# Loading the first slab of q's weights in two column halves, and x's first tile in two halves on two queues

## The chip, the cores and the metric

The kernel runs on one core of one Trainium2 chip. The metric is the time of one execution on the device in microseconds (us); the figure for a kernel is the median of several executions. Times such as "at 10.13" are us from the start of the profiled span.

The engines are named as the profile names them: PE multiplies matrices (PEld is its weight load), DVE, ACT and POOL work on vectors, SP only issues loads and stores. A name with q (SPq, ACTq) is that engine's instruction queue, in which DMA issues stand.

## The reference

Two branches work on `xn`, the layer-normed x of 2048 rows and 576 columns, and the result joins them:

```python
xn = layernorm(x)
q  = xn @ wq                       # 576 -> 32 heads of 128
p  = softmax(q @ k.T * Dh**-0.5)   # 16 key heads, last 512 rows of the caches
s  = (p @ v) @ wo                  # 4096 -> 576
h  = gelu(layernorm(xn) @ w1)      # its four quarters are shifted by 1, -1, 2, -2 rows
x1 = xn + shifted(h) @ w2
b  = x1 + gelu(layernorm(x1) @ w3) @ w4      # 576 -> 4608 -> 576
out = x + s * silu(b)
```

All arrays are bf16. `wq` has 576 rows and 4096 columns, `w4` 4608 rows and 576 columns.

## The kernel before

**Stages.** Rows go in four blocks of 512 (`QB`), a block is four tiles of 128 rows (`TB`). Stage A is attention with the first part of the second branch: a unit u is one head of one block, 128 units in all. For each unit PE makes q (`stage_q`, L460), the scores (`stage_s`, L481), their product with v (`stage_v`, L498), and the products with `wo`, `w1` and `w2` are placed between them. ACT takes the exponentials (L483), DVE copies and scales. Stage B, from about 539 us, is `w3`, GELU, `w4`: `up` (L894) and `down` (L931), over nine slabs of 512 columns of `w3` with the 512 rows of `w4` that belong to them (`load_w(i)`, L845 to L852). The order on PE, SP and POOL is written out by hand in both stages; for DVE and ACT it is so in the start and in stage B, and a planner sets it in the rest of stage A.

**The start.** All of this must be done before the first unit:

- x's first four tiles are loaded, two by SP and two by ACT (L316).
- `ln1_first` (L362 to L392) norms them. DVE takes mean and variance of tiles 0, 1 and 2 by `bn_stats` in two halves of 288 columns (L379). ACT takes those of tile 3 in two passes over it (L372, L373). Behind these two passes, in ACT's order, stands the square root for tiles 0 and 1 (L382); DVE's reciprocal (L389) needs it, and then applies the norm to each tile (L390).
- PE transposes the tiles (L404) and the first four key heads (L420), the transposes of a pair of tiles and of a pair of heads taking turns. DVE and ACT copy the five transposed chunks to `xT_b` (L410, L412): chunks 0, 1 and 4 DVE, chunks 2 and 3 ACT.
- `stage_q(0)` and `stage_q(1)` multiply them with the first two heads' weights, five matmuls each, one for each chunk of 128 rows of `wq` (the fifth has 64). A slab of `wq_b` holds four heads, 512 columns; `stage_q(2)` and `stage_q(3)` read its second half.

SP issues in this order: x tiles 0 and 1, key heads 0 and 1, key heads 2 and 3, the first slab of `wq` (L266, and its last 64 rows L269), v for two heads, the second slab of `wq`, v for two more heads, four more key heads. ACT issues x tiles 2 and 3 and then works.

**Semaphores of the loads.** Loads and stores issued by SP and ACT take eight semaphores in turn. In the trace each one from the ninth on waits, before it is issued, for the landing of the one that had its semaphore before: the first load of v waits for that of x's tile 2, the second for that of tile 0.

**From A to B.** `load_w` runs on SP from 511 us, each load behind such a wait or behind the release of memory that stage A used. For slabs 0 to 4 the 576 KB of `w4` come in one load, for slabs 5 to 8 in two. At the end of stage A ACT stores the last block of s (L544), also with one of the eight semaphores, then loads its table and takes the first GELU (L912).

Of the kernel before, what the change touches and what calls it, by code (L numbers as in the profile page):

```python
# [8 lines left out]
P = 128  # L9
# [22 lines left out]
def kernel(  # L32
# [14 lines left out]
    nc = tc.nc  # L47
# [3 lines left out]
    _, S, D = A_x.shape  # L51
    _, Hkv, Sk, Dh = A_k_cache.shape
# [13 lines left out]
    NF = D // P  # L66
    DR = D - NF * P
# [12 lines left out]
    x2 = A_x.rearrange("b s d -> (b s) d")  # L80
# [128 lines left out]
    with ExitStack() as actx:  # L209
# [9 lines left out]
        wq_b = [res.tile([P, NDC, 4 * Dh], BF16, name=f"wq_b{i}") for i in range(NWQ)]  # L219
# [26 lines left out]
        def x_tile(b):  # L246
            if b < 2:
                xt = hb_pool.tile([P, 5, QB + 2 * PAD], BF16, name="hb")[:].rearrange("p a b -> p (a b)")
            else:
                xt = x1_pool.tile([P, TB, D], BF16, name="x1")[:].rearrange("p a b -> p (a b)")  # L250
            return xt[:, 0:TB * D].rearrange("p (t d) -> p t d", t=TB)
# [10 lines left out]
        def load_wq(j, eng=None):  # L262
            eng = eng or nc.gpsimd
            w = wq_b[j % NWQ]
            c0 = (j % 8) * 4 * Dh
            eng.dma_start(out=w[:, 0:NF, :],  # L266
                              in_=A_wq[0:NF * P, c0:c0 + 4 * Dh].rearrange("(kc p) m -> p kc m", p=P))
            if j < PLAIN // 4:
                eng.dma_start(out=w[0:DR, NF, :], in_=A_wq[NF * P:D, c0:c0 + 4 * Dh])  # L269
                return  # L270
            last = A_wq[NF * P:D, c0:c0 + 4 * Dh].rearrange("p (j two m) -> p j two m", two=2, m=Dh)
            for k in range(2):
                eng.dma_start(out=w[k * DR:(k + 1) * DR, NF, 0:2 * Dh].rearrange("p (j m) -> p j m", j=2),
                              in_=last[:, :, k, :])
# [4 lines left out]
        def load_k(i, eng=None, step=4):  # L279
            kst_t[i] = x1_pool.tile([P, TB, D], BF16, name="x1")  # L280
            dst = kst_t[i][:].rearrange("p a b -> p (a b)")[:, 0:4 * W].rearrange("p (g a) -> p g a", g=4)
            for g in range(0, 4, step):
                (eng or nc.gpsimd).dma_start(
                    out=dst[:, g:g + step, :],
                    in_=A_k_cache[0, 4 * i + g:4 * i + g + step, K0:, :].rearrange("g (p kc) d -> p g (kc d)", p=P))

        def load_v(i, eng=None):
            for g in (2 * i, 2 * i + 1):
                (eng or nc.gpsimd).dma_start(out=v_sb[:, g, :, 0:Dh],
                                             in_=A_v_cache[0, g, K0:, :].rearrange("(p kc) d -> p kc d", p=P))  # L290
# [20 lines left out]

        x_t[0] = []
        x_first = x_tile(0)
        for tt in range(TB):
            xt = x_first[:, tt, :]
            (nc.sync if tt < 2 else nc.scalar).dma_start(out=xt, in_=x2[tt * P:(tt + 1) * P, :])  # L316
            x_t[0].append(xt)
        for w in (xn_b[0], xnn_b):
            nc.gpsimd.memset(w[:, :, D:], 0.0)
# [1 line left out]
            nc.gpsimd.memset(w[DR:, NF, :], 0.0)  # L321
        with tc.manual_schedule(engines={SP}):
            load_k(0, nc.sync, 2)
            load_wq(0, nc.sync)
            load_v(0, nc.sync)
            load_wq(1, nc.sync)
            load_v(1, nc.sync)
            load_k(1, nc.sync)
# [466 lines left out]
        with tc.manual_schedule(engines={SP, POOL, PE}):  # L795
            for u in range(0, max(max(fill), max(pe_fill)) + 1):
                atoms = pe_fill.get(u, []) + [fn for v, g in pe_late if v == u for fn in prep_k(g)]
                n = len(atoms)
# [23 lines left out]
    with ExitStack() as bctx:  # L822
# [5 lines left out]
        WS = 4  # L828
# [14 lines left out]
        def load_w(i):  # L843
            c0 = i * WS * P
            nc.sync.dma_start(out=w3_s[i][:, :, :],  # L845
                              in_=B_w3[0:NF * P, c0:c0 + WS * P].rearrange("(kc p) f -> p kc f", p=P))
            last = B_w3[NF * P:D, c0:c0 + WS * P].rearrange("p (j two m) -> p j two m", two=2, m=P)
            for k in range(2):
                nc.sync.dma_start(out=w3r_s[i][k * DR:(k + 1) * DR, :, :], in_=last[:, :, k, :])
            for k in range(0, WS, WS if i < 5 else WS // 2):  # L850
                n = WS if i < 5 else WS // 2
                nc.sync.dma_start(out=w4_s[i][:, k:k + n, :],  # L852
                                  in_=B_w4[c0 + k * P:c0 + (k + n) * P, :].rearrange("(fc p) d -> p fc d", p=P))

        with tc.issue_after(last_t[0].ins):
            for i in range(NSL):
                load_w(i)
# [236 lines left out]
        with tc.manual_schedule(engines={PE, DVE, ACTE, SP}):  # L1094
# [20 lines left out]
            tt = TB - 1  # L1115
# [11 lines left out]
    with tc.If(flag > 0):  # L1127
        nc.sync.dma_start(out=g_dram[(NT - 1) * P:NT * P, :], in_=g_last)
        with ExitStack() as gctx:
# [19 lines left out]
            with tc.For_i(0, NT, 1) as t:  # L1149
                tok = bass.ds(t * P, P)  # L1150
                xt = work.tile([P, D], BF16, name="r_x")
# [8 lines left out]
                for h in range(Hq):  # L1160
                    g = h // REP
                    if h % REP == 0:
                        k_nat = work.tile([P, KCH, Dh], BF16, name="r_k")
                        nc.sync.dma_start(out=k_nat[:],
                                          in_=A_k_cache[0, g, K0:, :].rearrange("(kc p) d -> p kc d", p=P))
                        v_g = work.tile([P, KCH, Dh], BF16, name="r_v")
                        nc.sync.dma_start(out=v_g[:],
                                          in_=A_v_cache[0, g, K0:, :].rearrange("(kc p) d -> p kc d", p=P))
# [16 lines left out]
                    p = work.tile([P, W], BF16, name="r_p")  # L1185
# [63 lines left out]
```

## Time and profile before

| | |
|---|---|
| three executions | 829.02, 829.21, 830.68 us |
| median | 829.21 us |
| the profiled execution | 829.95 us, of it the span 828.2 us |
| PE busy | 819.9 us, 99% of the span |
| granted PE clock | full in all 40 slices |
| DVE, ACT, POOL busy | 472.4, 456.0, 96.1 us |
| DMA | 83.81 MB, 101 GB/s over the span |

The profile is of one execution. "Idle before" is the time in which an engine did nothing before an instruction, with what ended it. The chain of work is followed back from the last instruction; time of an engine that is not on the chain costs nothing by itself.

The trace has a landing mark for each DMA from each of the 16 DMA engines; a load has landed when the last has come. In the start these are, issue to landing:

| load | queue | issued | landed |
|---|---|---|---|
| x tile 0 | SP | 0.75 | 3.50 |
| x tile 2 | ACT | 0.75 | 3.72 |
| x tile 1 | SP | 1.21 | 4.16 |
| x tile 3 | ACT | 1.19 | 4.37 |
| keys of heads 0, 1 | SP | 1.68 | 7.78 |
| keys of heads 2, 3 | SP | 2.15 | 8.59 |
| first slab of wq | SP | 2.67 | 10.09 |
| its last 64 rows | SP | 3.18 | 10.48 |
| v, two heads | SP | 3.80, 4.44 | 10.88, 11.48 |
| second slab of wq | SP | 5.12 | 14.07 |

From the keys on one of the 16 engines is behind the rest: 15 had finished the keys of heads 0 and 1 by 6.01 and the first slab of wq by 8.60.

### The profile page before, as it was taken

To read this page: it belongs to the slowest core of one execution; us is meant where nothing else is said; L and a number is where in the kernel's file an instruction comes from. 1 tells how busy PE (TensorE), PEld (TensorE's weight loads), DVE (VectorE), ACT (ScalarE), POOL (GpSimd) and SP (SyncE) were. 2 spreads that over 40 slices of the span, in tenths; PEclk is the share of its full clock that TensorE was granted. 3 is DMA by queue.
4 is the path that set the end of the run, shared out by engine and by line. 5 is a ranking of instruction groups with operands and counts; after the bars stand their busy time and mean duration, and the time that the engine had idled before them with its cause. 6 is when DMAs were issued, how large, how long until landed. Compare 5 with 4: busy or idle time off the path is not lost.

```text
span 828.2 us, 19604 instructions
## 1 busy us (share of the span) xinstructions
PE 819.9 (99%) x7974; PEld 470.0 (57%) x7974; DVE 472.4 (57%) x1431; ACT 456.0 (55%) x821; POOL 96.1 (12%) x163
## 2 busy tenths in 40 slices
PE   8999999999999999999999999999999999999997
PEld 5666654655564565655466555555555555555555
DVE  5878645678885357964346774044246626645323
ACT  7888853588773368984457983033233423334610
POOL 4353223010100111110001100000000000000000
PEclk9999999999999999999999999999999999999999
DMA  7998992263472145762045454992000311220101
GB/s 196 196 189 175 192 171 76 80 125 71 107 140 56 42 91 125 139 137 49 13 81 128 103 106 94 314 332 42 2 16 30 91 44 45 48 87 16 45 15 40
DMA packets 141217, 83.81 MB, mean 101 GB/s; under 512 B 107888, under 2 KB 134000, under 8 KB 141120
## 3 DMA queue, kind: packets, MB, share of 16 engines
q1 hardware_dynamic: 130464, 53.01, 32.1%
q0 software_dynamic: 9408, 28.15, 12.9%
q8 instruction: 64, 1.05, 0.5%
q10 hardware_dynamic: 1248, 1.33, 0.5%
q14 instruction: 33, 0.27, 0.1%
HBM read 49.17 MB, written 9.29 MB: 71 GB/s over the span
## 4 chain that ended last, share of the span: by engine, by line
PE 98%; DMA 1%; ACT 0%; SPq 0%; DVE 0%; issue 0%; ACTq 0%
PE po L498 14%; PE ph L894 14%; PE psq L460 13%; PE sc L481 13%; PE pswo L522 13%; PE pm L931 11%; PE pm L1101 4%; PE ph L574 3%; PE pm L894 2%; PE psx L625 2%; PE pswr L522 2%; PE pr L931 2%; PE psq L445 1%; DMA wq_b<-in_A_wq_dram 1%; PE sc L445 1%; PE pr L1101 0%
## 5 line engine op out<-in xcount | busy, mean ns | idle before, releaser
L483 ACT ACTIVATE pT<-sc 128x512 bf16<-128x512 f32 x512 | 285.3, 598 | 104.9 <-PE sc L481 98.2
L481 PE MATMUL sc<-qT,kT 128*128 128x512 bf16 x512 | 172.8, 379 | 0.0
L498 PEld LDWEIGHTS <-pT 128*128 128x128 bf16 x2048 | 134.4, 98 | 55.0 <-issue 10.6
L498 PE MATMUL po<-v_sb,pT 128*128 128x129 bf16 x2048 | 158.3, 220 | 0.1
L460 PE MATMUL psq<-xT_b,wq_b 128*128 128x512 bf16 x516 | 132.0, 379 | 0.7 <-DMA wq_b<-in_A_wq_dram 0.7
L894 PE MATMUL ph<-xT_b,w_s 64*128 64x512 bf16 x976 | 127.1, 376 | 0.0
L931 PE MATMUL pm<-w_s,h 64*128 64x512 bf16 x864 | 122.3, 377 | 0.0
L522 PE MATMUL pswo<-wo_sb,oT 128*128 128x512 bf16 x512 | 116.5, 379 | 0.0
L503 DVE TENSOR_TENSOR o<-po,ri_b 128x256 bf16<-128x256 f32 x256 | 108.0, 422 | 6.4 <-DVE ri_b L502 0.3
L912 ACT ACTIVATE h<-ph 128x512 bf16<-128x512 f32 x67 | 39.4, 597 | 130.3 <-PE ph L894 130.3
L931 PEld LDWEIGHTS <-h 64*128 64x128 bf16 x1728 | 70.8, 94 | 55.5 <-issue 0.4
L522 PEld LDWEIGHTS <-oT 128*128 128x128 bf16 x1024 | 65.3, 98 | 56.7
L931 PE MATMUL pr<-w_s,h 64*128 64x64 bf16 x864 | 90.2, 189 | 0.2 <-ACT h L912 0.2
L894 PEld LDWEIGHTS <-w_s 64*128 64x128 bf16 x1152 | 57.2, 94 | 48.3 <-issue 0.2
L460 PEld LDWEIGHTS <-wq_b 128*128 128x128 bf16 x516 | 50.1, 98 | 60.1 <-issue 1.3
L910 DVE COPY hx<-ph 128x512 f32<-128x512 f32 x55 | 38.1, 692 | 69.3 <-PE ph L894 69.3
L502 DVE RECIPROCAL ri_b<-po 128x2 f32<-128x2 f32 x256 | 42.2, 165 | 50.3 <-PE po L498 46.3
L481 PEld LDWEIGHTS <-kT 128*128 128x128 bf16 x512 | 47.0, 98 | 26.6 <-DVE qT L468 0.6
L468 DVE TENSOR_TENSOR qT<-psq,rq 128x512 bf16<-128x512 f32 x62 | 42.8, 690 | 26.7 <-ACT pT L483 19.7
L266 POOL DMA_DIRECT2D wq_b<-in_A_wq_dram x30 | 23.2, 774 | 292.1 <-PE sc L481 292.1
L470 DVE CAST qT<-psq 128x512 bf16<-128x512 f32 x42 | 28.9, 689 | 34.3 <-PE psq L445 29.2
L884 DVE TENSOR_SCALAR fence<-ph,ph 1x1 f32<-1x1 f32 x61 | 12.8, 210 | 51.2 <-PE ph L894 50.6
(152 smaller groups left out, 749.5 us busy)
## 6 DMA issues: line engine op xcount, KB each, us to landing
wq_b<-in_A_wq_dram POOLq DMA_DIRECT2D x30, 512.0 KB, 4.7
wo_sb<-in_A_wo_dram POOLq DMA_DIRECT2D x8, 576.0 KB, 5.3
w_s<-in_B_w_dram SPq DMA_DIRECT2D x9, 512.0 KB, 7.3
w_s<-in_B_w_dram SPq DMA_DIRECT2D x5, 576.0 KB, 7.0
x_dram<-x SPq DMA_DIRECT2D x4, 576.0 KB, 3.4
x<-x_dram SPq DMA_DIRECT2D x4, 576.0 KB, 4.1
w_s<-in_B_w_dram SPq DMA_DIRECT2D x8, 288.0 KB, 5.2
s_b<-s_dram SPq DMA_DIRECT2D x4, 576.0 KB, 4.9
```

Of the source, the lines that this page charges most:

```text
L460: nc.tensor.matmul(psq[:, :], lhsT=w[:, kc, hh * Dh:(hh + 1) * Dh], rhs=xT_b[qb % 2][:, kc, :], start=(kc == 0 and not (two and hh == 1)), ...
L468: nc.vector.tensor_tensor(out=qT[:, :], in0=psq[:, :], in1=rq_t.pop(u)[:, :], op=ALU.add)
L481: nc.tensor.matmul(sc[:, :], lhsT=kT[:, g, kc * P:(kc + 1) * P], rhs=qT_t[u][:, :], start=True, stop=True)
L483: nc.scalar.activation(out=pT[:, :], in_=sc[:, :], func=ACT.Exp, scale=SCALE)
L498: nc.tensor.matmul(po[:, j, :], lhsT=pTs[kc][:, tt * P:(tt + 1) * P], rhs=v_sb[:, g, kc, 0:Dh + 1], start=(kc == 0), stop=(kc == KCH - 1))
L502: nc.vector.reciprocal(out=ri, in_=po[:, :, Dh])
L503: nc.vector.tensor_tensor(out=o[:, t0:t0 + 2, :], in0=po[:, :, 0:Dh], in1=ri.unsqueeze(2).to_broadcast([P, 2, Dh]), op=ALU.mult)
L522: nc.tensor.matmul(ps, lhsT=oT_t[qb * Hq + h][:, tt, :], rhs=wo_sb[:, h, lo:hi], start=(h == 0), stop=(h == Hq - 1))
L894: nc.tensor.matmul(ps[i][:, :], lhsT=lhsT, rhs=xT[half, kc, :], start=first, stop=last, skip_group_check=True)
L910: nc.vector.tensor_copy(out=src[:, :], in_=ps[i][:, :])
L912: nc.scalar.activation(out=h3[:, :], in_=src[:, :], func=ACT.Gelu_apprx_tanh)
L931: nc.tensor.matmul(out, lhsT=h3_t[b, fc][half, tt * P:(tt + 1) * P], rhs=w4_s[fc // WS][half, fc % WS, lo:hi], start=key not in started, s ...
```

## The change

Three places are changed. The right half (columns 288 to 575) of x's tile 0 is issued by ACT, ahead of tiles 2 and 3; SP's load of tile 0 keeps the left half. The first slab of `wq` is loaded as columns 0 to 255 and then columns 256 to 511, each with its last 64 rows behind it, so four loads in place of two, with rows of 512 bytes in place of 1024. In stage B the `w4` rows of slabs 5, 6 and 7 come in one load each instead of two; slab 8 keeps two.

```diff
         x_first = x_tile(0)
+        hw = D // 2
+        nc.scalar.dma_start(out=x_first[:, 0, hw:D], in_=x2[0:P, hw:D])
         for tt in range(TB):
             xt = x_first[:, tt, :]
-            (nc.sync if tt < 2 else nc.scalar).dma_start(out=xt, in_=x2[tt * P:(tt + 1) * P, :])
+            n = D if tt else hw
+            (nc.sync if tt < 2 else nc.scalar).dma_start(out=xt[:, 0:n], in_=x2[tt * P:(tt + 1) * P, 0:n])
             x_t[0].append(xt)
...
             load_k(0, nc.sync, 2)
-            load_wq(0, nc.sync)
+            for m0 in (0, 2 * Dh):
+                cols = slice(m0, m0 + 2 * Dh)
+                nc.sync.dma_start(out=wq_b[0][:, 0:NF, cols],
+                                  in_=A_wq[0:NF * P, cols].rearrange("(kc p) m -> p kc m", p=P))
+                nc.sync.dma_start(out=wq_b[0][0:DR, NF, cols], in_=A_wq[NF * P:D, cols])
             load_v(0, nc.sync)
...
-            for k in range(0, WS, WS if i < 5 else WS // 2):
-                n = WS if i < 5 else WS // 2
+            for k in range(0, WS, WS if i < 8 else WS // 2):
+                n = WS if i < 8 else WS // 2
                 nc.sync.dma_start(out=w4_s[i][:, k:k + n, :],
                                   in_=B_w4[c0 + k * P:c0 + (k + n) * P, :].rearrange("(fc p) d -> p fc d", p=P))
```

## The prediction

> **What bounds the kernel now.** First the page: by the chain that ended last, PE alone sets the time.
>
> ```profile
> PE 98%; DMA 1%; ACT 0%; SPq 0%; DVE 0%; issue 0%; ACTq 0%
> ```
>
> So a load is worth only what PE waits for it. The waits of PE are read next; these four are all that the view has (us in total, times, longest):
>
> ```profile
> PE warm L774 <- POOL ident masks.py:199: 1.6, 1, 1.6
> PE psq L460 <- DMA wq_b<-in_A_wq_dram: 0.7, 1, 0.7
> PE warm L777 <- DVE ln_mv L383: 0.3, 1, 0.3
> PE pr L931 <- ACT h L912: 0.2, 1, 0.2
> ```
>
> The reader sees that one wait of 0.7 us belongs to a load that the change touches, and that no wait in stage B belongs to `w4`. The chain of waits in the first 16 us places it (start, length, what):
>
> ```profile
> 2.67 7.42 DMA wq_b<-in_A_wq_dram
> 10.09 0.05 issue
> 10.13 2.33 PE psq L460 x10
> ```
>
> The first q matmul starts when the slab has landed. What would stop it next is in the timeline of the start:
>
> ```profile
> 0.75 0.90 ACTq L316 DMA_DIRECT2D hb<-in_A_x_dram  x2
> 0.75 0.88 SPq L316 DMA_DIRECT2D hb<-in_A_x_dram  x2
> ...
> 4.39 0.68 ACT L372 ACTIVATE wo_sb<-hb 128x576 f32<-128x576 bf16 x1 [1.21 <-DMA hb<-in_A_x_dram]
> ...
> 5.97 0.28 ACT L382 ACTIVATE nr_y<-ln_mv,eps_t 128x2 f32<-128x2 f32 x1
> ...
> 6.37 0.16 DVE L389 RECIPROCAL nr_y<-nr_y 128x2 f32<-128x2 f32 x1
> ...
> 8.98 1.08 ACT L410 ACTIVATE xT_b<-ps_x 128x512 bf16<-128x512 bf16 x2 [0.63 <-PE ps_x L404]
> ```
>
> Two things are to be seen. The last transposed chunk from ACT is ready at 8.98 + 1.08 = 10.06, only 0.03 before the slab. And the norm hangs on two chains that end nearly together: DVE's statistics of tiles 0 to 2 (3.52 to 6.44), and ACT's passes over tile 3, which begin at 4.39 when that tile lands; the square root behind them ends at 6.25, and DVE's reciprocal starts at 6.37.
>
> **Part 1, the halves of wq.** Loads on SP's queue land in order, held by the slow DMA engine: keys of heads 2 and 3 at 8.59, the slab 1.50 later, its last rows at 10.48, the two v loads 0.40 and 0.60 after that. The 1.50 is for 512 rows of 1024 bytes; a v load is 512 rows of 256 bytes, 0.50 in the mean. 512 rows of 512 bytes lie between; by length, 0.50 + 1.00 x 256/768 = 0.83. I take that, since both neighbours are loads of the same queue, one behind the other. The first half then lands at 8.59 + 0.83 = 9.42, its last rows by 9.7; the bounds are 9.1 and 10.09. The second half would land at about 10.6, or 11.7 by the upper bound, and `stage_q(2)` reads it at 13.16: covered. The v loads move by no more than the extra 0.2 to 1.6 us, to 11.1 to 13.1 against a first use at 14.68.
>
> With the weights there, PE is free at 9.45 (end of the key transposes, 8.84 + 0.61). Chunks 0, 1 and 2 are ready by then or just after, chunk 3 at 10.06. So matmul 4 starts at 10.10, matmul 5 0.22 later, and it ends 0.38 after its start: 10.70. Today the five start at 10.13 in steps of 0.22 and the fifth ends at 11.37. The part is worth 0.67 us at most, because the transposed x is then what is late. Everything after it up to 17 us (DVE's copy of q, scores, exponentials) starts from these matmuls, and the chain stays on PE, so the gain is kept.
>
> Its added waits: with the extra loads the eight semaphores go round sooner. The last rows of the first half wait for ACT's half tile (about 3.5, where they were issued at 3.18), the second half for SP's half tile, the second slab for the keys of heads 0 and 1: 7.78 where it was issued at 5.12. Behind that on SP stand two v loads, four key heads and the first transpose of o at 16.68. The second slab landed at 14.07 and is first read at 19.32; on the slow engine its data come after v (11.5) either way. Cost nothing; if the 5.2 us of cover were gone, up to the 2.7 us by which its issue is later.
>
> **Part 2, the halves of x's tile 0.** SP's half has half the bytes. From SP's first tile to its second the landing moves 0.66 (3.50 to 4.16), so half a tile less is up to 0.3 earlier; the first `bn_stats` reads just these 288 columns and would start at 3.2 to 3.5. ACT's half is first in its queue and smaller than the tile that landed at 3.72: about 3.5, before DVE's second `bn_stats` needs it. DVE's statistics end up to 0.3 earlier. This is worth nothing, because the reciprocal also needs ACT's square root, which has 6.37 - 6.25 - 0.05 = 0.07 to spare (0.05 is the step from matmul 5's end at 11.37 to DVE's cast at 11.42).
>
> That square root stands behind tile 3, and tile 3 is now ACT's third load instead of its second. One issue on ACT takes 0.41 to 0.47 in the row above (two in 0.90). The lower end is nothing: x's four tiles have the same bytes in sum, and tile 3 was already the last. The upper end is one issue and a key load that gets its turn ahead: 256 KB at the 370 GB/s that the DMA view shows for 3 to 4 us, 0.7, so 1.1. I take 0.4, the ACT queue's own row. ACT's table load, 1.68 to 2.96, also moves back 0.45 and stays hidden before 4.39. Then ACT's passes, the square root, the reciprocal, the norm, the transposes and the copies all move by 0.4 - 0.07 = 0.33, and matmul 5 with them.
>
> [...]
>
> **Part 3, w4 in one load.** Three issues fewer on SP, of 0.4 to 0.6 each. Slab i is first read about 544.2 + 3.93 i (the pairs of `up` and `down` repeat every 3.93: 548.28, 552.21, 556.14), so slab 5 at 563.9. Its halves landed at 541.0 and 542.9; one load of 576 KB takes 7.0 in the median against 5.2, from an issue at 534.87 to 536.4, so 543.5 at the latest. 20 us of cover: nothing. Without the cover, 1.8 for each slab. The order of landings here matters at one other place:
>
> ```profile
> 540.04 0.89 SPq L852 DMA_DIRECT2D w_s<-in_B_w_dram  x2
> ...
> 540.24 0.39 ACTq L544 DMA_DIRECT2D s_dram<-hb  x1
> ...
> 540.95 1.28 ACT L912 ACT_TABLE_LOAD   x1 [1.28 <-DMA w_s<-in_B_w_dram]
> ...
> 542.45 0.60 ACT L912 ACTIVATE h<-ph 128x512 bf16<-128x512 f32 x1 [0.21 <-PE ph L894]
> ```
>
> ACT was free at 539.67, but its store waited for the semaphore that a load of slab 5's last rows of `w3` held until 540.17. The table load ended at 542.23, 0.22 before the first GELU could start. With two loads fewer ahead of it the store should fall on slab 5's main `w3` load (landed 539.97): 0.2 earlier, hidden, worth nothing.
>
> **Sum.** -0.67 + 0.33 = -0.34 us. Against the profiled execution: span 828.2 to 827.9, time 829.95 to 829.6. That execution lay 0.74 above the median, so the median goes from 829.21 to 828.9.
>
> **Rivals.**
> A. The forecast, with tile 3 between 0 and 0.7 late and the half slab anywhere in its bounds: -0.67 to 0, 828.5 to 829.2.
> B. Tile 3 also falls behind a key load: 1.1 late, so -0.67 + 1.03 = +0.36, 829.6. [...]
> C. Tile 3's share on the slow engine falls behind the keys there, which land at 7.78. The mark follows the data by about 0.5 (the last x packets end at 3.91, the last mark is at 4.37), so the keys' data end at 7.3 and ACT starts about 2.9 late: -0.67 + 2.83 = +2.2, 831.4, slower. It decides from tile 3 landing after 6.7. Against: the slow engine stands idle before its keys, it is not busy with them, and ACT's queue could use it.
> D. ACT's store of s falls on the semaphore of slab 5's undivided `w4` load, which lands at about 542.9: the table load moves 2.7, the first GELU 2.5, and PE waits for it: 831.4, slower. It decides from a landing 0.22 later than 540.17. Against: it needs the store to stand three places further behind in the order of the loads, and only two loads are taken out ahead of it.
> E. The halves of wq land no sooner because short rows cost as much as long ones (10.09): the delay of tile 3 and the slab then overlap, 0 to +0.4, 829.2 to 829.6.
>
> **How the numbers follow.** A 0.49, B 0.18, C 0.06, D 0.05, E 0.13; 0.09 stays for a different order of DVE and ACT in stage A from the planner, and scatter, in either direction. 0.2%, 1.66 us, is about what a measurement of this kernel tells from no change: its three executions lie that far apart. A, B and E are within it (0.80), and of the rest 0.01 too: same 0.81. C and D are slower, 0.11, with 0.03 of the rest: 0.14. Faster than 827.5 needs a wait that PE does not have in this trace, so only the rest can give it: 0.05. The time is A's, 828.9; A's own range with the scatter of two of the three executions (0.2) is 828.3 to 829.4. For 8 in 10 the range takes in B and E with the run that lay 1.5 above its fellows, and C and D at 831.4; below, 0.67 and as much again for scatter: 828.0 to 831.4.
>
> **What would show it.** Right: PE's wait for `wq_b` is gone and the first q matmul starts at 9.4 to 9.9; matmul 5 ends near 11.0; ACT's first pass over tile 3 starts at 4.8; DVE's first `bn_stats` at 3.2 to 3.5; the loads of slabs 5 to 7 appear once each and no wait of PE in stage B names them. Wrong: ACT's first pass after 5.2 (B) or after 6.7 (C); ACT's store at 542 or later and a PE wait for h beyond 0.2 (D); the wait for `wq_b` still there (E); new waits of PE on ACT or DVE between 20 and 530 us (the planner).

## The result: 2.7 us slower, in two places that the sum had at 0.33 and at nothing

The changed kernel takes 831.91 us (median of 8 executions, 830.98 to 833.43), the kernel before 829.22 beside it (8 executions). The ratio is 1.0032, 95% interval 1.0021 to 1.0043: slower, by more than the 0.2% that separates a difference from none here, and above the predicted range, which ended at 831.4. The profiled execution took 831.61, its span is 829.8.

The page of the changed kernel gives its chain almost wholly to PE, as before, so again only what PE waits for counts:

```profile
PE 97%; DMA 1%; ACT 0%; DVE 0%; issue 0%; ACTq 0%; SPq 0%
```

The waits of PE (us in total, times, longest):

```profile
PE warm L781 <- POOL ident masks.py:199: 1.6, 1, 1.6
PE ps_x L411 <- DVE xn_b L397: 1.4, 1, 1.4
PE pswo L529 <- DMA oT<-o: 0.9, 1, 0.9
PE pr L938 <- ACT h L919: 0.2, 1, 0.2
```

The wait for `wq_b` is gone, as predicted. Two waits are new: 1.4 us in the start, for the normed x, and 0.9 us for the last transpose of o, 500 us later, at the handover from stage A to B. The chain in the first 16 us now begins with a tile of x, where it began with the slab of `wq`:

```profile
1.68 4.38 DMA hb<-in_A_x_dram
6.06 0.02 issue
6.09 0.79 ACT wo_sb L379 x2
...
8.67 0.79 PE ps_x L411 x10
```

This load is tile 3, ACT's third. It is issued at 1.68 instead of 1.19 and lands at 6.06 instead of 4.37, so ACT's first pass over it starts at 6.09 (4.39 before). The timeline shows what follows on the other engines:

```profile
6.09 0.68 ACT L379 ACTIVATE wo_sb<-hb 128x576 f32<-128x576 bf16 x1 [2.42 <-DMA hb<-in_A_x_dram]
...
7.98 0.17 DVE L396 RECIPROCAL nr_y<-nr_y 128x2 f32<-128x2 f32 x1 [0.93 <-ACT nr_y L389]
...
8.67 0.79 PE L411 MATMUL ps_x<-ident,xn_b 128*128 128x128 bf16 x10 [1.35 <-DVE xn_b L397]
```

DVE's reciprocal starts at 7.98 (6.37 before): it had been done with the statistics and waited 0.93 for ACT. The five q matmuls end at 12.18.

At the handover the timeline of the kernel before shows PE's matmuls with `wo` without a break, the last transpose of o on SP, and the instructions of POOL and SP behind it:

```profile
507.73 10.52 PE L522 MATMUL pswo<-wo_sb,oT 128*128 128x512 bf16 x48
...
508.72 1.21 SPq L511 DMA_TRANSPOSE oT<-o  x1
...
509.51 0.59 POOL L662 DMA_DIRECT2D mx_dram<-m  x1 [31.25 <-DVE m L661]
510.86 0.37 SPq L197 DMA_DIRECT2D x<-x_dram  x1
```

In the changed kernel the matmul that needs the transpose waits for it:

```profile
509.50 1.23 SPq L518 DMA_TRANSPOSE oT<-o  x1
510.28 0.59 POOL L669 DMA_DIRECT2D mx_dram<-m  x1 [31.24 <-DVE m L668]
...
512.62 0.37 SPq L197 DMA_DIRECT2D x<-x_dram  x1
516.22 2.71 PEld L529 LDWEIGHTS <-oT 128*128 128x128 bf16 x14 [1.36 <-DMA oT<-o]
516.22 2.98 PE L529 MATMUL pswo<-wo_sb,oT 128*128 128x512 bf16 x13 [0.87 <-DMA oT<-o]
```

The transpose lands 6.67 us after its issue; before it was 2.76. PE would begin the matmul that reads it 5.70 us after the issue, as it did before, and begins it 6.72 after: 1.02 are lost. The idle time in the view is smaller, 0.87, because PE starts such a matmul every 0.22 us while the record of each is 0.38 long.

The table divides the spans, in us. Since the start of before's profiled execution was late by a wait that the other profiles don't have (next section), the kernel with only `w4` undivided (e9), which ran as before does in the median, stands beside it.

| part | before | e9 | after |
|---|---|---|---|
| to the end of the fifth q matmul | 11.38 | 10.54 | 12.18 |
| from there to the first `w3` matmul | 527.80 | 527.79 | 528.82 |
| stage B on PE | 283.55 | 283.50 | 283.50 |
| behind PE's last | 5.45 | 5.52 | 5.34 |

Against e9 the changed kernel loses 1.64 in the start and 1.03 at the handover, and gains 0.18 at the end: 2.49, where the medians lie 2.69 apart.

### The profile page after: what moved, and what is told of

Its sections match the earlier page's. It is cut to its first block, busy times and chain, and to the rows that moved or that the text cites. A ratio compares the mean times of both kernels' runs of the same rounds, so it can differ in the third digit from the quotient of the medians.

```text
span 829.8 us, 19604 instructions
## 1 busy us (share of the span) xinstructions
PE 820.4 (99%) x7974; PEld 470.6 (57%) x7974; DVE 472.7 (57%) x1431; ACT 456.4 (55%) x821; POOL 96.3 (12%) x163
## 4 chain that ended last, share of the span: by engine, by line
PE 97%; DMA 1%; ACT 0%; DVE 0%; issue 0%; ACTq 0%; SPq 0%
PE po L505 14%; PE ph L901 14%; PE psq L467 13%; PE sc L488 13%; PE pswo L529 13%; PE pm L938 11%; PE pm L1108 4%; PE ph L581 3%; PE pm L901 2%; PE psx L632 2%; PE pswr L529 2%; PE pr L938 2%; PE psq L452 1%; PE sc L452 1%; DMA oT<-o 1%; DMA hb<-in_A_x_dram 1%
```

## The experiments

All are medians of 6 to 11 executions. The ratios come from all executions, not from the medians, against 17 to 33 executions of before on the same chip. Some of these took 830 to 836, except beside e17 and e18; so e10's ratio is 1.0000 though its median is 1.0 above the 829.29 of before there, and e5's interval holds 1 though its median is 1.06 above 829.13. "+2.76" is the landing of the last transpose of o, in us after its issue.

| run | edit | median | ratio, 95% | fifth q matmul ends | last transpose | PE waits for it |
|---|---|---|---|---|---|---|
| e1 | no halves of x | 830.20 | 1.0013 [1.0004, 1.0022] | 10.53 | +6.26 | 0.46 |
| e2 | halves of x alone | 831.40 | 1.0027 [1.0015, 1.0039] | 11.96 | +2.77 | no |
| e3 | after, tile 2 on SP | 829.10 | 0.9992 [0.9974, 1.0010] | 10.53 | +5.62 | no |
| e4 | after, more warming | 831.29 | 1.0027 [1.0017, 1.0037] | 11.76 | +6.47 | 0.67 |
| e5 | before, SP 2 longer | 830.19 | 1.0009 [0.9998, 1.0020] | 10.54 | +6.42 | 0.61 |
| e6 | e1, one v pair on POOL | 829.48 | 1.0004 [0.9995, 1.0013] | 10.73 | +5.81 | no |
| e7 | e3, v and keys on POOL | 829.78 | 1.0008 [0.9999, 1.0017] | 10.49 | +5.71 | no |
| e8 | after, tile 3 ahead of tile 2 | 829.94 | 1.0012 [1.0003, 1.0022] | 10.86 | +6.23 | 0.42 |
| e9 | w4 undivided alone | 829.26 | 0.9995 [0.9986, 1.0004] | 10.54 | +2.74 | no |
| e10 | before, late start | 830.27 | 1.0000 [0.9985, 1.0016] | 11.87 | +2.74 | no |
| e11 | e2, more warming | 831.22 | 1.0021 [1.0012, 1.0030] | 12.31 | +2.76 | no |
| e12 | before, SP 3 shorter | 829.83 | 1.0004 [0.9995, 1.0013] | 11.07 | +5.59 | no |
| e13 | e1, loads held back | 829.43 | 0.9997 [0.9981, 1.0012] | 10.95 | +5.16 | no |
| e14 | before, loads held back | 829.99 | 1.0011 [1.0002, 1.0020] | 10.78 | +2.75 | no |
| e15 | e3, loads held back | 829.78 | 1.0009 [1.0000, 1.0018] | 10.19 | +4.75 | no |
| e16 | before, SP 8 longer | 828.88 | 1.0007 [0.9996, 1.0019] | 10.57 | +2.76 | no |
| e17 | e1, small store behind | 829.49 | 1.0004 [0.9995, 1.0013] | 10.53 | +3.33 | no |
| e18 | after, small store behind | 832.01 | 1.0033 [1.0020, 1.0045] | 13.72 | +3.35 | no |

### Which part costs what: e1, e2, e9

e1 is the change with x's tiles loaded as before:

```diff
-        hw = D // 2
-        nc.scalar.dma_start(out=x_first[:, 0, hw:D], in_=x2[0:P, hw:D])
...
-            n = D if tt else hw
-            (nc.sync if tt < 2 else nc.scalar).dma_start(out=xt[:, 0:n], in_=x2[tt * P:(tt + 1) * P, 0:n])
+            (nc.sync if tt < 2 else nc.scalar).dma_start(out=xt, in_=x2[tt * P:(tt + 1) * P, :])
```

> The changed kernel with x's tile 0 loaded whole by SP again (the halves of wq and the undivided w4 loads stay). Theory 1, tile 3 is late because it is third in ACT's queue: ACT's first pass starts at 4.4 again, the first half slab lands near 9.4, PE's wait for wq_b is gone, 828.5 us. Theory 2, the extra loads of wq (short rows, semaphores used up sooner) hold tile 3 back: ACT's first pass stays after 5, 831 to 832 us.

e2 is before with these lines the other way, e9 before with `i < 8` for `i < 5` in the loads of `w4`.

> The kernel before with the halves of x's tile 0 alone. Theory 1: tile 3 lands near 6.0, first q matmul near 10.9, 831.5 to 832.5 us, with a scatter as wide as that of the changed kernel. Theory 2: tile 3 lands before 4.9, at most 829.6 us.

> The kernel before with the undivided w4 loads of slabs 5 to 7 alone. All theories: no wait of PE in stage B names w4, ACT's store of s is issued between 540 and 541, within 0.3 us of 829.1 us.

In e1 ACT's first pass starts at 4.39 again, as theory 1 has it, but its 828.5 is missed by 1.7. The halves of x cost 2.2 (831.40 against 829.19), the halves of `wq` 1.0 (830.20), `w4` nothing (829.26 against 829.29). The two add up to 3.2, together they cost 2.7.

e9 also answers what the halves of `wq` could win. It loads the slab whole. These are the first three of the four lines of its waits of PE:

```profile
PE warm L774 <- POOL ident masks.py:199: 1.6, 1, 1.6
PE warm L777 <- DVE ln_mv L383: 0.3, 1, 0.3
PE ps_x L404 <- DVE xn_b L390: 0.2, 1, 0.2
```

No wait for `wq_b`: the slab lands at 8.34, its last rows at 8.63, and the q matmuls start at 9.17, when the transposed x is there. e1, with halves, also starts them at 9.17. The profiles of e5, e14 and e16, which load the slab whole too, have no such wait either. The wait of 0.7 that the forecast took away belonged to one execution, in which one DMA engine ran 1.5 to 1.8 us behind the others.

### Where x's third tile in ACT's queue loses its time: e3, e8

```diff
-            (nc.sync if tt < 2 else nc.scalar).dma_start(out=xt[:, 0:n], in_=x2[tt * P:(tt + 1) * P, 0:n])
+            (nc.scalar if tt == 3 else nc.sync).dma_start(out=xt[:, 0:n], in_=x2[tt * P:(tt + 1) * P, 0:n])
```

> The changed kernel with x's tile 2 issued by SP, third there, so that ACT has the right half of tile 0 and then tile 3. Theory 1: tile 3 lands near 4.2, DVE's reciprocal starts near 6.1 (0.3 before the kernel before, because DVE's statistics start at 3.0), 828.2 to 828.6 us. Theory 2: tile 3 lands after 5 and the time stays above 830.5 us.

With tile 2 on SP, tile 3 is ACT's second load again:

```profile
4.39 0.68 ACT L379 ACTIVATE wo_sb<-hb 128x576 f32<-128x576 bf16 x1 [1.21 <-DMA hb<-in_A_x_dram]
...
9.17 2.44 PE L467 MATMUL psq<-xT_b,wq_b 128*128 128x512 bf16 x9
```

ACT's pass starts at 4.39 and the start is that of before, with x's tile 0 in halves all the same. So the halves themselves cost nothing there, and win nothing (829.10 against the forecast 828.2 to 828.6); the place in the queue costs. e8 gives tile 3 ACT's second place and tile 2 the third.

> The changed kernel with ACT's loads in the order right half of tile 0, tile 3, tile 2. Theory 1, the third place in ACT's queue is late whatever stands there: tile 3 lands near 4.2, tile 2 near 5.8, DVE's third statistics start at 5.8 instead of 5.0 and its reciprocal near 6.9 instead of 8.0, 830.5 to 831.2 us. Rival, tile 3 is late for itself: it lands after 5 again, 831.9 us.

Tile 3 landed at 4.50 and tile 2 at 5.66: the third place is late, whichever tile has it. The third load of the other queue is not: in e3 tile 2, SP's third, was also issued at 1.68 and landed at 4.61. In the changed kernel SP's third load is that of keys 0 and 1, issued at 1.68 beside ACT's third; their first landing marks come at 4.91 and 4.65, their last at 6.32 and 6.06. The two go side by side, and x's 144 KB are done only when most of the keys' 256 KB are. That the keys are the reason is read from these landings; no run moved the keys. e8's landings are near those of theory 1, its time is better than forecast (829.94 against 830.5 to 831.2).

### Whether PE's idle time adds to it: e4, e10, e11

PE idles 1.35 us before the transposes of the changed kernel. e4 fills this with 24 more warming matmuls (`warm(29)` for `warm(5)`), e11 does so in e2; e10 makes before late by the same means (`warm(31)`).

> The changed kernel with 24 warm-up matmuls more on PE just before its first transposes, which fill the 1.4 us in which it waits there. No theory has tile 3 sooner. If PE's waiting also costs granted clock after it, and that is the scatter of 2.5 us between executions: the scatter shrinks to about 1 us and the median falls to 830.5 to 831. If the scatter comes from the loads alone: 831.9 us and 2.5 us of scatter stay.

> The kernel with the halves of x's tile 0 alone, and the 24 more warm-up matmuls. If PE's idle time before the transposes costs granted clock in some executions: 830.4 to 830.9 us instead of 831.4, and less scatter than 2.8 us. If not: 831.4 us as without them.

> The kernel before with 26 warm-up matmuls more on PE ahead of its first transposes, so that its start is late by about 1.4 us with PE at work and with no load changed. If a late start costs its own length and no more: 830.5 us, the last transpose lands within 3 us. If a late start by itself also pushes the last transpose behind SP's instruction load: more than 831 us and a wait for that transpose.

e11's forecast was missed: 831.22 against e2's 831.40, so idling doesn't explain the median. e4's 831.29 lies between its two forecasts, 0.6 below the changed kernel, and the two intervals overlap. What narrows is the scatter: 830.8 to 831.9 against 830.5 to 833.3, and 830.9 to 832.4 in e4 against 831.0 to 833.4. e10 shows that a start 1.33 us late costs 1.0, and that lateness does not push the last transpose (+2.74).

### What delays the last transpose: e5, e6, e7, e12, e16

e5 is before with one pair of v loads in four pieces, two more instructions in SP's queue and nothing else.

```diff
-            load_v(1, nc.sync)
+            for g in (2, 3):
+                for k in (0, 2):
+                    nc.sync.dma_start(out=v_sb[:, g, k:k + 2, 0:Dh],
+                                      in_=A_v_cache[0, g, K0:, :].rearrange("(p kc) d -> p kc d", p=P)[:, k:k + 2, :])
```

> The kernel before with one edit that touches neither x nor wq: v for heads 2 and 3 comes in four loads on SP instead of two, so that SP's program is two instructions longer, as the halves of wq make it. Theory 3, the longer program of SP moves its instruction-block load (511.2 us) onto the last transpose of o, and a DMA engine that is behind after such a load delays that transpose: it lands 5 to 7 us after its issue instead of 2.8, PE waits for it 0.5 to 1 us, 829.7 to 830.3 us. Rival, the wait comes from the halves of wq or from the start being earlier or later: no wait, 829.2 us.

Its waits of PE name the transpose, and its median is as far above before (1.06) as e1's (1.01):

```profile
PE pswo L525 <- DMA oT<-o: 0.6, 1, 0.6
```

So `wq` is not needed for it; two more instructions are enough. e6 and e7 take instructions off SP again, by giving `load_v(1)`, and in e7 `load_k(1)` as well, to POOL; e12 does the latter in before.

> The kernel with halves of wq and undivided w4 (x whole), with v for heads 2 and 3 issued by POOL, so that SP's program is as long as before up to the last transpose. Theory 3: the last transpose lands within 3 us, no wait for it, and what the halves of wq give in the start is left, 828.4 to 829.0 us. Rival: the wait of 0.5 us and about 830.2 us stay.

> The changed kernel with x's tile 2 on SP as its third load, and v for heads 2 and 3 and the key heads 4 to 7 issued by POOL, so that SP's program is as long as before. Theories 1 and 3: tile 3 lands near 4.3, the last transpose within 3 us, 828.2 to 828.9 us. If the start is bound by the norm in both kernels, no better than 829.1.

> The kernel before with v for heads 2 and 3 and the key heads 4 to 7 issued by POOL, so that SP's program is three instructions shorter up to the last transpose. Theory 3: SP's instruction load comes more than 2.5 us after the issue of the last transpose, which then always lands within 3 us; 828.8 to 829.1 us, scatter not above that of the kernel before. Rival: as 829.1 or more.

PE hardly waited any more (in e6 its matmul began 0.15 late), but the transpose still landed at +5.6 to +5.8, with SP's count as before in e6 and e7 and with three instructions fewer in e12. All three missed their forecasts; of e12's excess, 0.53 is in the start (11.07). These three are no clean test of SP's length, since they give the loads to POOL, whose queue also issues the small store of the next table. With eight more on SP the transpose was early again:

> Before, with eight more DMA instructions on SP's queue in the start (the last v and key loads in smaller pieces). Theory 'shared engines': what matters is whether the transpose finishes before packets of x1 come; which way it falls at this length can't be told beforehand, but landing over +5.8 and a wait of PE go together: without one 829.2, with one 829.8 to 830.3. Rival 'SP's program': the longer, the later, a wait of more than 0.6 and over 830.2.

In e16 it landed at +2.76, and the kernel ran at 828.88. The length of SP's program therefore doesn't decide by itself. In all of these kernels, before and after included, one thing goes with the landing: the order of the transpose and POOL's store of `m` (L662 of before, 128 rows of 8 bytes, issued 0.8 us behind the transpose). The landing marks, first to last, in us after the issue of the transpose:

| | transpose | store of `m` |
|---|---|---|
| before | 2.55 to 2.76 | 2.75 to 5.70 |
| e16 | 2.60 to 2.76 | 2.78 to 5.53 |
| after | 3.42 to 6.67 | 3.26 to 6.51 |
| e5 | 3.53 to 6.42 | 3.37 to 6.24 |
| e6 | 2.79 to 5.81 | 2.64 to 5.60 |
| e12 | 3.00 to 5.59 | 2.72 to 5.38 |

Where the transpose finishes first it is early; where the store has come in front, each of the transpose's 16 marks, in order of time, comes 0.15 to 0.29 behind one of the store's. The store itself takes 3.8 to 5.7 us from its issue to its last mark.

### The store or the loads behind: e13, e14, e15, e17, e18

Behind the transpose SP also issues the load of x1 (L197) and `w3`. e13 holds these back in e1, by a store of 2 bytes that waits for the transpose; e14 and e15 do it in before and in e3.

```diff
+            last_t[0] = nc.sync.dma_start(out=hold[:, :], in_=oT_t[U - 1][0:1, 0, 0:1])
...
         with tc.issue_after(last_t[0].ins):
+            load_x1(1)
             for i in range(NSL):
```

> Halves of wq and undivided w4, x's tiles as before, and on SP, behind the last transpose of o, one store of 2 bytes that reads its result. So the load of x1 (rows of 1152 bytes) and the loads of w3 and w4 are issued only after that transpose has landed. Without the store: 830.20 us, the transpose lands 6.3 us after its issue, PE waits 0.46. Theory 'shared engines': the transpose is late because packets of the load of x1 get onto the engines before it has finished; held back, it lands at most 3.6 after its issue, PE waits for nothing there, 829.2 us. Rival 'SP's program': two more instructions make the transpose itself slow, whatever follows it; it lands 5.5 or more after its issue and PE still waits 0.4: 830.2.

> Before, with only that store behind the last transpose of o. The price of the store by itself: the loads behind it start some 2 us later, 20 us before stage B reads them. Both theories: transpose at +2.5 to +2.8 as before, 829.2, no wait of PE at the handover. If the store itself costs, over 829.6.

> The change with x's tile 2 on SP's queue (829.10, transpose at +5.62, no wait seen in its profile), and the store behind the last transpose. Theory 'shared engines': transpose by +3.6, and 829.0 to 829.2, since PE did not wait there in the profile without the store either. Rival 'SP's program': the same time, transpose at +5.5 or later.

Both theories of e13 failed in part: PE's wait went and the time with it (829.43 against 830.20), but the transpose landed at +5.16, not at +3.6, and the first packets of x1 came only at +6.9. The loads add about 1.1 of the delay (+6.26 in e1); most of it was there without them. e14's forecast was missed as well: holding back costs 0.9 in before. Of that its profile has 0.35 in stage B (283.85) and 0.6 behind PE's last (6.06). 0.2 of the 0.35 is a wait of PE for DVE's copy `hx`, which e13, e15, e17 and e18 have too; what makes the rest was not followed. e15 paid 0.7 (829.78 against 829.10), with the transpose at +4.75.

e17 leaves the loads and puts the small store behind the transpose, by a copy on POOL that waits for it:

```diff
+            nc.gpsimd.tensor_copy(out=gate[:, :], in_=oT_t[U - 1][0:1, 0, 0:1])
             nc.gpsimd.dma_start(out=mx_dram[:, :], in_=m2[:])
```

> Halves of wq and undivided w4, x's tiles as before (830.20, last transpose at +6.26, wait 0.46), and on POOL, ahead of the store of m (128 rows of 8 bytes), a copy of one element that waits for the last transpose of o. The loads of x1 and w3 on SP are issued as they were. Theory 'behind the small store': in all kernels with a late transpose its marks come 0.15 to 0.3 after those of this store, engine by engine, and in all with an early one before them. Put behind, the store can't hold it: the transpose lands at +3.6 or earlier, no wait of PE, 829.1 to 829.3. Rival 'load of x1': the packets of x1 from +4.2 on hold it: it lands at +5 or later, with or without the store.

The timeline of e17 has the transpose, the load of x1 at its usual place, then the copy and the store:

```profile
507.81 1.22 SPq L515 DMA_TRANSPOSE oT<-o  x1
510.92 0.37 SPq L197 DMA_DIRECT2D x<-x_dram  x1
511.26 0.18 POOL L666 COPY gate<-oT 1x1 bf16<-1x1 bf16 x1 [33.92 <-DMA oT<-o]
511.74 0.59 POOL L667 DMA_DIRECT2D mx_dram<-m  x1 [0.30 <-issue]
```

The transpose lands at +3.33, all 16 marks within 0.14 us, and PE's matmuls with `wo` run through. The time is 829.49, 0.7 below e1 and 0.3 above before; stage B is 0.42 longer in this kernel (283.92). So the store in front of the transpose is the cause of its late landing. The load of x1 is where it was in e1, and so is an 8 KB load of instructions, 1.8 us behind the issue of the transpose in both: neither holds the transpose without the store. What is left above +2.76 is 0.57.

The packets in the traces show what is late. In every run the transpose's own packets begin between 1.4 and 2.7 us after its issue, and those of x1's load no sooner than 3.1. The data are moved in time; the marks come late.

How the store gets in front is read from the packets and was not tested by itself. In before the last packet of the transpose begins at 2.25 and the first of the store at 2.26. In after, e1, e4, e5, e8 and e13, with two more instructions on SP, the load of instructions falls at 1.8 instead of 2.5, the transpose's packets go on until 2.67 to 2.69, and the store's begin at 2.25 to 2.28, ahead of the last of them. In e16 that load falls 7.1 us ahead of the transpose, and the packets are as in before.

The transpose and the store are on different queues (q1 and q0 in the DMA view of the changed kernel), and in the late runs the mark of the one follows that of the other by 0.15 to 0.29, as far as marks that are paired by their order in time can show it. Why it follows is not shown.

> The whole change with the same copy ahead of the store of m. Theory 'behind the small store': the transpose lands at +3.6 or earlier, no wait of PE for it, the 1.0 of the handover goes: 830.9 to 831.1 instead of 831.9; the start stays late (ACT's first pass at 5.6 to 6.2). Rival 'load of x1': transpose at +5 or later, 831.4 or more.

In the whole change the wait also goes: +3.35, and 527.77 from the q matmuls to stage B instead of 528.82. But the median did not fall (832.01, six executions from 830.42 to 834.33), so what the store costs in the whole change is shown by the profile and not by the time. Its profiled execution lost as much elsewhere: 0.43 in stage B and 1.54 in the start. Its windows (span; busy us and instructions of PE, PEld, DVE, ACT, POOL; granted clock; DMA share; GB/s) show where:

```profile
8.00:10.00 2.00, 1.25 (x18) 1.19 (x19) 1.77 (x6) 1.71 (x4) 0.00 (x0) 0.88 1.12 228
10.00:12.00 2.00, 2.00 (x21) 2.00 (x20) 0.92 (x3) 0.70 (x2) 0.00 (x0) 0.50 1.17 308
12.00:14.00 2.00, 2.00 (x11) 0.85 (x9) 0.41 (x2) 1.36 (x3) 0.00 (x0) 0.76 1.21 268
```

Behind an idle stretch of PE from 6.90 to 8.76 the granted clock was at a half from 9.53 to 12.95. In the changed kernel's own profile PE idled from 7.32 to 8.67 and the clock stayed full.

No version beat before: the best were e16 and e3, at 828.88 and 829.10, with intervals that hold 1.

## Why the prediction was wrong

**What bounds the kernel.** Right in the way of reading, wrong in one line of it. PE sets the time and only its waits count. But the wait of 0.7 for `wq_b` was no property of the kernel. The text had both signs in hand, the one slow DMA engine and the 0.74 by which that execution lay above the median, and still took the wait as what the median pays.

**Part 1, -0.67.** This step failed first. The half slab does land sooner (8.00, its last rows at 8.29; forecast 9.42 and 9.7), but the whole slab is there at 8.63 in e9, before it is needed at 9.17. The term is nothing.

**"Cost nothing" for the added waits.** The cover that was named, the second slab and v, held: PE waits for neither. Not looked at was the other end of SP's queue, 500 us later. Two more instructions change how the last transpose of o and a small store of POOL come in, and PE needs that transpose 5.70 after its issue. The measured term is +1.0 by the medians of e1 and e5; the profiles of e1, e5 and after have the matmul 0.61, 0.76 and 1.02 late.

**Part 2, +0.33.** The mechanism was right, the size of one term not: the lateness of tile 3. DVE's first `bn_stats` starts at 2.97, somewhat before the forecast 3.2 to 3.5, and it is worth nothing, as said. Tile 3 is 1.69 late instead of 0.4: its row was ACT's issue (0.49 later, as the trace has it), and the rest, 1.20, is lost side by side with the keys (last landing marks at 6.06 and 6.32). This is rival B's mechanism, put at 1.1 and 829.6. The 0.07 to spare was right: DVE's reciprocal is 1.61 late. ACT's first pass at 6.09 is past the 5.2 that was to tell B. The start loses 1.64 against e9, and the part alone costs 2.2, of which 0.5 stands behind PE's last in both profiles (6.07 in e2, 6.05 in e11); where that comes from stays open.

**Part 3, nothing.** Right: 829.26 against 829.29, and no wait of PE in stage B names `w4`. The step of 3.93 us from slab to slab was only half of the true one, though: in before, PE first reads the `w4` of slabs 4 and 5 at 575.79 and 583.65, 7.86 apart, so slab 5 is first read 20 us later than the 563.9 of the working, and the cover was 40 us instead of 20.

**The rivals.** D did not happen: ACT's store of s went at 541.52 and the wait for h is 0.2 as before. C's mark, a first pass after 6.7, was not reached. E is right in that the halves of `wq` bring nothing, for another reason: the whole slab is early enough.

**Sum with the measured terms.** 0 for `wq`, +1.6 in the start and +1.0 at the handover, against -0.67, +0.33 and 0: 2.6 of the 2.7. The chances failed at two points: slower was given 0.14, for C, D and a part of the rest. B stood among the outcomes with no difference, since its delay was put at 1.1; the halves of x alone make the kernel slower (e2, 1.0027). And no rival looked at the handover.

## What to carry to other kernels

Before a wait in one profiled execution is put in a sum, ask whether the median has it: an execution above the median with one DMA engine behind is a reason to look for the second-latest operand, and to price the gain at nothing as one end. Where two queues of loads are filled early, as here, look at which load stands beside a small one that the start hangs on: ACT's third landed 1.7 us later beside the keys on SP, and moving it to SP ahead of the keys won that back (e3: ACT's first pass at 4.39 instead of 6.09). And an instruction added to a queue can be felt far down that queue's program, here 500 us later (the transpose at +6.42 in e5, at +2.76 before): look at where PE next depends on a transfer of it with little slack, and at small stores to DRAM that other engines issue just beside it.

## What was not expected of the hardware

- A store of 128 rows of 8 bytes to DRAM lands 3.8 to 5.7 us after its issue, its marks spread over 1.7 to 3.3 us; in e17 and e18, issued 3.2 us later, it takes 7.9 and 7.5. A transpose of 128 KB that comes behind it is late with it, though on another queue and with its own packets in time: +4.75 to +6.67 instead of +2.74 to +2.77.
- What decides the order is small. Where the 8 KB load of instructions falls at 1.8 (after, e1, e4, e5, e8, e13) or 0.3 us ahead of the issue (e3, e15) the transpose was late; where it falls at 2.5 it was early in before, e2, e9, e10, e11 and e14 and late in e6, e7 and e12, the three that give loads to POOL. There the packets of the two meet within 0.03 us, as in before (e6: last of the transpose 2.27, first of the store 2.24). Why these three differ stays open.
- After a similar idle of PE, the granted clock fell to 0.50 for 3.42 us in e18 (idle of 1.86) and stayed full in after (1.35) and e2 (2.1). What sets the one apart from the others is not shown. The narrower scatter of e4 and e11 (1.5 and 1.1 us, against 2.4 in after and 2.8 in e2) fits a cost of idling, but a single profile shows the drop.
